# A gated mix of a state-space convolution and a GLU: the planner orders the queues with another timing model

## The chip, the cores and the metric

The kernel runs on one core of a Trainium2 chip. The metric is the device time of one execution in microseconds, from three runs of the kernel before: 757.71, 754.04 and 754.38, median 754.38. A core has five engines, each with a queue of its own that it works through in order: TensorE (PE in the profile; PEld is its loading of weights), VectorE (DVE), ScalarE (ACT), GpSimd (POOL) and SyncE (SP), which here issues every DMA transfer.

## The reference

The input `x` has 2048 positions (L) of 512 channels (D). Two branches are computed from it and mixed with a gate.

```
g = sigmoid((x * gate_w).sum(-1, keepdims=True))          # one number per position

# branch A: a convolution with a kernel built from a state space
dt = exp(log_dt)[:, None]                                 # 512 x 1
P  = exp((dt * (A_re + 1j*A_im))[:, :, None] * l)         # 512 x 128 x 2048, l = 0..2047
K  = einsum("dn,dnl,dn->dl", C_re + 1j*C_im, P, dt * (B_re + 1j*B_im)).real
y  = irfft(rfft(pad(x)) * rfft(pad(K)))[:2048] + x * Dskip   # per channel

# branch B: a GLU with 1792 hidden units
h  = sigmoid(x @ w_gate) * (x @ w_up)                     # 2048 x 1792
b  = h @ w_down                                           # 2048 x 512

out = g * y + (1 - g) * b
```

## The kernel before, in words

Branch A is done as matrix products in two stages, so that a transform of 4096 points becomes products with small constant matrices. Branch B is a plain chain of two matrix products whose operands are each split into a high and a low part (three products for one), for precision.

**kgen** (lines 191 to 241) builds the convolution kernel K in 16 rounds of 32 channels. A round takes the bases of the powers (`bases`, lines 147 to 178: products on VectorE, and Exp and Sin on ScalarE, lines 162 to 172), writes the first powers into the tile `T` (lines 200 to 204; `T` has one buffer, so a round can write it only when the `kps` products of the round before have read it), and then doubles the table of powers again and again (`double`, lines 180 to 189). A doubling is three operations on VectorE: two products (lines 187 and 188) and a sum (line 189), up to 128 x 2048 elements each. When the table is full, 128 small products on TensorE (line 220, tile `kps`) sum over the states, ScalarE copies the result (line 223, `kst`), VectorE adds Dskip (line 225), 32 products (line 232) make the first transform stage, and ScalarE copies these out (line 236). Every fourth round stores its result (line 239).

**rows** (lines 354 to 371) runs 16 times, once for each block of 128 positions. It loads the block, computes the gate (lines 360 to 362) and does the first transform stage of x on TensorE (line 367), which goes to a buffer in memory (line 371).

**glu** (lines 303 to 352) is a generator of the whole of branch B, so that the other parts can draw work from it in portions. It goes through two halves of the positions, four groups of hidden tiles (4, 4, 3 and 3 tiles of 128 units), two blocks of 512 positions. `load_x` (line 304) loads and splits x; `weights` (line 373) loads and splits one hidden tile's weights (casts on ScalarE, lines 381 and 382; low parts on VectorE, lines 384 and 385, stored for the second half in lines 386 and 387 and read back in lines 389 and 390); four weight tiles are held (`bufs=4`). `hidden` (line 393) makes one hidden tile for 512 positions: 24 products on TensorE (line 401) into two of three `gups` buffers, then a sigmoid on ScalarE (408), a product on VectorE (409), a cast on ScalarE (410) and the low part on VectorE (411). The second products (line 339) sum a group's hidden tiles into `dps`, and ScalarE or VectorE adds this to an accumulator (lines 343 and 345).

**finish** (lines 252 to 285) is the second transform stage in 16 passes: it loads four tiles (lines 255 to 261), makes products with the transformed x and with the transformed kernel (line 248), multiplies them (lines 268 and 269), combines and moves the parts (lines 274 to 278), makes the inverse products (line 281) and stores the result (line 284). **final** (lines 287 to 297) runs 16 times: it loads a block back, does the last stage (line 293), mixes it with branch B (line 296) and stores the output.

The program text (lines 426 to 457) interleaves these parts by hand-set step counts: `ROW` = 32 portions of `glu` for every four `rows`, `MID` = 50 for every half round of `kgen`, `END` and `LAST` for `finish` and `final`.

That text is not yet the order on the queues. The tile context collects all instructions and then plans them when its block closes: it plays the program through on a timing model, and at each moment gives an engine an instruction whose inputs are ready and whose buffers are free, and among those the one that stands first in the program text. Lines 214 to 240, from the `kps` products to the store, are raised above this with `tc.high_priority()`. The order in which the planner hands out the instructions is the order in which they stand on each engine's queue; on the chip each then waits for its own inputs. The timing model's times serve for this order alone.

## Time and profile before

| | |
|---|---|
| median of three runs | 754.38 us |
| the profiled execution | 753.36 us |
| its span, first to last instruction | 751.6 us |
| mean granted TensorE clock | 0.975 of full speed |
| instructions in the profile | 12658 |
| `kps` products, first and last start | 64.4 and 547.9 us |
| first products of `finish` (line 248) on the chain | 565.21 us |

The page gives busy times of each engine over the span. A fp32 matrix product appears as more than one record. The windows view gives, for stretches of the span, busy time and count of instructions of each engine, the granted TensorE clock, the share of DMA time and GB/s; asked for one source line it gives that line's instructions alone. The lines view groups instructions by source line and form: busy time and mean duration, then idle time of that engine just ahead of them, with what ended it. The chain that ended last gives in order of time the start, the length and the name of each piece that set the end. The waits view gives who waited for whom. A row named SPq is the DMA-issuing queue of SyncE.

### The profile page before, as it was taken

What the parts mean: (1) busy time and instruction counts of PE and PEld (TensorE: products, weight loads), DVE (VectorE), ACT (ScalarE), POOL (GpSimd) and SP (SyncE); (2) the same over time, 40 slices, a digit from 0 to 9 for tenths busy, and PEclk for the clock granted to TensorE, in tenths of its full rate; (3) what the DMA queues carried; (4) which work ended last, traced back from release to release, by engine and by line L of the source; (5) the groups of instructions that cost most, each with busy time, mean ns of one, the idle gap of its engine ahead of it and who ended that gap; (6) DMA issues with size and microseconds to landing.
All of it is one profiled execution on the core that took longest, in us unless ns stands there. A gap on an engine that the chain in (4) does not pass through costs nothing.

```text
span 751.6 us, 12658 instructions
## 1 busy us (share of the span) xinstructions
PE 706.8 (94%) x5024; PEld 475.2 (63%) x5024; DVE 604.9 (80%) x835; ACT 375.5 (50%) x611; POOL 3.7 (0%) x36
## 2 busy tenths in 40 slices
PE   4988889998999999999999999999999999999995
PEld 3445348877888778877787787887883323333651
DVE  5888989999999999899999898999944544454343
ACT  5364645763638274655565654546134555555200
POOL 0000000000000000000000000000000000000000
PEclk9789879999999999999999999999999999999999
DMA  6768662433025033565013350531158877774587
GB/s 221 213 204 229 170 178 97 156 104 148 32 88 183 22 115 130 194 237 175 26 57 126 100 189 8 168 115 56 57 187 284 258 241 243 225 223 147 174 285 254
DMA packets 61019, 118.64 MB, mean 158 GB/s; under 512 B 8224, under 2 KB 22944, under 8 KB 59936
## 3 DMA queue, kind: packets, MB, share of 16 engines
q1 hardware_dynamic: 60960, 117.84, 48.3%
q8 instruction: 39, 0.64, 0.3%
q14 instruction: 20, 0.16, 0.1%
HBM read 75.35 MB, written 42.47 MB: 157 GB/s over the span
## 4 chain that ended last, share of the span: by engine, by line
PE 53%; DVE 28%; ACT 8%; DMA 7%; issue 3%; SPq 0%; DVEq 0%; ACTq 0%
PE gups L401 19%; PE dps L339 12%; PE fps L248 9%; DVE T L189 6%; DVE T L188 6%; DVE tmp L187 6%; PE ips L281 4%; PE fps L367 3%; DVE h L409 2%; PE kps L220 2%; DVE hl L411 2%; DMA xs<-xt 2%; PE fps L232 2%; DMA wst<-wgu 1%; PE fps L293 1%
## 5 line engine op out<-in xcount | busy, mean ns | idle before, releaser
L401 PE MATMUL gups<-xh,gu 128*128 128x512 f32 x896 | 293.9, 402 | 15.2 <-ACT gu L381 12.5
L401 PEld LDWEIGHTS gups<-xh,gu 128*128 128x128 f32 x896 | 170.0, 191 | 71.4 <-issue 16.2
L401 PE MATMUL gups<-xl,gu 128*128 128x512 f32 x448 | 179.2, 400 | 0.0
L339 PE MATMUL dps<-dnw,hh 128*128 128x512 f32 x448 | 150.2, 402 | 3.6 <-ACT hh L410 3.0
L187 DVE TENSOR_TENSOR tmp<-T,bz 128x64 f32<-128x64 f32 (+2 forms) x96 | 114.8, 1195 | 2.3 <-issue 0.2
L189 DVE TENSOR_TENSOR T<-T,tmp 128x64 f32<-128x64 f32 (+2 forms) x96 | 114.6, 1194 | 0.7
L188 DVE TENSOR_TENSOR T<-T,bz 128x64 f32<-128x64 f32 (+2 forms) x96 | 114.6, 1193 | 0.0
L339 PEld LDWEIGHTS dps<-dnw,hh 128*128 128x128 f32 x448 | 83.5, 189 | 37.5 <-issue 11.6
L401 PEld LDWEIGHTS gups<-xl,gu 128*128 128x128 f32 x448 | 85.6, 191 | 27.4 <-issue 10.3
L339 PE MATMUL dps<-dnw,hl 128*128 128x512 f32 x224 | 89.6, 401 | 3.0 <-DVE hl L411 1.7
L408 ACT ACTIVATE sg<-gups 128x512 f32<-128x512 f32 x56 | 33.5, 598 | 70.3 <-PE gups L401 69.6
L268 DVE TENSOR_TENSOR t<-fps,uf 128x512 f32<-128x512 f32 x32 | 22.0, 688 | 57.6 <-PE fps L248 47.6
L410 ACT ACTIVATE hh<-h 128x512 fp32r<-128x512 f32 x56 | 35.1, 628 | 47.9 <-DVE h L409 47.9
L409 DVE TENSOR_TENSOR h<-gups,sg 128x512 f32<-128x512 f32 x56 | 38.1, 684 | 20.4 <-PE gups L401 20.1
L339 PEld LDWEIGHTS dps<-dnw,hl 128*128 128x128 f32 x224 | 42.3, 189 | 16.5 <-DVE hl L411 3.7
L411 DVE TENSOR_TENSOR hl<-h,hh 128x512 fp32r<-128x512 f32 x56 | 38.3, 686 | 8.9 <-ACT hh L410 8.4
L381 ACT ACTIVATE gu<-wst 128x1024 fp32r<-128x1024 f32 x28 | 29.6, 1057 | 29.4 <-PE gups L401 13.8
L345 DVE SCALAR_TENSOR_TENSOR acc<-dps,omg,acc 128x512 f32<-128x512 f32 x48 | 35.5, 746 | 10.3 <-PE dps L339 10.3
L248 PE MATMUL fps<-au,w_in 128*64 128x512 f32 x128 | 42.3, 611 | 0.3 <-DVE t L268 0.3
L236 ACT ACTIVATE kev<-fps 128x256 f32<-128x256 f32 x64 | 33.8, 678 | 16.3 <-PE fps L232 15.4
L248 PE MATMUL fps<-ak,w_in 128*64 128x512 f32 x128 | 41.2, 609 | 0.0
L367 PE MATMUL fps<-u,wu 64*128 64x512 f32 x64 | 32.4, 780 | 6.6 <-DMA u<-xp 2.9
(78 smaller groups left out, 664.5 us busy)
## 6 DMA issues: line engine op xcount, KB each, us to landing
wst<-wgu SPq DMA_DIRECT2D x28, 512.0 KB, 4.5
a_u<-evu SPq DMA_DIRECT2D x32, 256.0 KB, 3.3
a_k<-kev SPq DMA_DIRECT2D x8, 1024.0 KB, 6.0
au<-a_u SPq DMA_DIRECT2D x16, 512.0 KB, 4.8
ak<-a_k SPq DMA_DIRECT2D x16, 512.0 KB, 4.2
b_s<-evb SPq DMA_DIRECT2D x32, 256.0 KB, 2.5
b_in<-b_s SPq DMA_DIRECT2D x16, 512.0 KB, 4.6
wsd<-wdn SPq DMA_DIRECT2D x28, 256.0 KB, 3.5
```

The lines of the kernel that those rows point to most:

```text
L187: nc.vector.tensor_tensor(t2, src, sb, op=OP.mult)
L188: nc.vector.tensor_tensor(dst, src, br, op=OP.mult)
L189: nc.vector.tensor_tensor(dst, dst, t2[:, :, ::-1], op=OP.add)
L236: nc.scalar.activation(kv[i][:, s:s + 4], p4[:, :, :, 16 * i:16 * i + 16], AF.Copy)
L248: mm(p[64 * kb:64 * kb + 64], w[:, kb, 64 * c:64 * c + 64], a(kb), start=True, stop=True, tile_position=(0, 64 * kb), skip_group_check=True)
L339: mm(p, a[:, hs], dnw[:, b], start=(n == 0), stop=(n == last))
L345: nc.vector.scalar_tensor_tensor(accs[t], p, omg[:, t:t + 1], accs[t], op0=OP.mult, op1=OP.add)
L367: mm(ph[jp], wu[r, jp], u[r], start=True, stop=True, tile_position=(64 * jp, 0))
L401: mm(p, gu[:, a, k, dc], b[:, dc], start=(n == 0), stop=(n == 11))
L409: nc.vector.tensor_tensor(h, pp[1], sg, op=OP.mult)
L410: nc.scalar.activation(hh, h, AF.Copy)
L411: nc.vector.tensor_tensor(hl, h, hh.bitcast(F32), op=OP.subtract)
```

## The change

The tile context gets an argument that sets the timing model with which it plans. Without it, the planner uses a simple model with one cost for each instruction and transfer. With it, it uses a more detailed model, in which an instruction passes through its queue, its engine and the end of its writes one after another, and transfers through issue, start and data. Ranking, dependencies, buffers, the instructions themselves and what they compute stay as they are; the order on every queue, and with it the waits between them, can be another.

```
-    with tile.TileContext(nc) as tc, ExitStack() as ctx:
+    with tile.TileContext(nc, schedule_with_timeline_sim=True) as tc, ExitStack() as ctx:
         body(ctx, tc, *args)
```

## The prediction

> **What bounds the kernel now.** I read the page's totals first, then the busy times of three stages, then the chain that ended last for the pitch of each kind of product, then the waits.
>
> ```profile
> span 751.6 us, 12658 instructions
> PE 706.8 (94%) x5024; PEld 475.2 (63%) x5024; DVE 604.9 (80%) x835; ACT 375.5 (50%) x611; POOL 3.7 (0%) x36
> ```
>
> TensorE carries the span, but busy is not the same as working at full pitch. The stages come from the windows view (columns: stretch, its length, busy time of each engine with its instruction count, granted clock, DMA share): the head with the 16 `rows` steps, the middle with most of `kgen`, and the end with `finish` and `final`.
>
> ```profile
> 0.00:125.00 125.00, 100.40 (x587) 59.51 (x588) 105.93 (x183) 62.18 (x123) 0.84 (x10) 0.86 0.66 194
> 125.00:550.00 425.00, 414.30 (x3772) 335.75 (x3773) 408.86 (x515) 234.10 (x356) 2.82 (x26) 1.00 0.33 112
> 550.00:751.60 201.60, 192.06 (x672) 79.92 (x666) 90.07 (x138) 79.25 (x132) 0.00 (x0) 0.99 0.71 232
> ```
>
> The middle is a double bound: TensorE 414 and VectorE 409 of 425 us. In the end VectorE needs only 90 of 201.6 us. The same view for the GLU's products alone, line 401 first and line 339 second:
>
> ```profile
> 0.00:125.00 125.00, 46.28 (x155) 32.33 (x156) 0.86 0.66 194
> 125.00:550.00 425.00, 244.18 (x1032) 192.07 (x1031) 1.00 0.33 112
> 550.00:751.60 201.60, 45.42 (x158) 28.11 (x158) 0.99 0.71 232
> ...
> 0.00:125.00 125.00, 14.76 (x48) 9.31 (x48) 0.86 0.66 194
> 125.00:550.00 425.00, 128.27 (x516) 94.66 (x516) 1.00 0.33 112
> 550.00:751.60 201.60, 29.33 (x108) 19.42 (x108) 0.99 0.71 232
> ```
>
> The chain, in order of time (start, length, what), gives the pitch of undisturbed runs of products:
>
> ```profile
> 77.52 1.47 PE fps L367 x4
> 399.35 1.92 PE kps L220 x128
> 402.64 1.97 PE fps L232 x32
> 449.97 4.08 PE dps L339 x18
> 565.21 3.81 PE fps L248 x16
> 574.32 1.09 PE ips L281 x2
> 720.23 1.87 PE fps L293 x8
> ```
>
> So one GLU product takes 4.08/18 = 0.2267 us, and its 1344 + 672 = 2016 of them 457.0 us. The others: 16 rounds of `kps` at 1.92 (30.7) and of L232 at 1.97 (31.5), 64 of L367 at 0.3675 (23.5), 256 of L248 at 0.238 (61.0), 64 of L281 at 0.545 (34.9), 64 of L293 at 0.234 (15.0). Together 653.6 us, so 98 us of the span are lost by TensorE. By stage: the head has 203 GLU products (46.0), L367 (23.5) and two rounds of `kgen` (7.8), 77.3 of 125, and loses 47.7. The middle has 1548 (350.9) and 14 rounds (54.5), 405.4 of 425, and loses 19.6. The end has 266 (60.3) and 110.9 of `finish` and `final`, 171.2 of 201.6, and loses 30.4. A new order can win or lose only in these 98 us and in what it adds to them.
>
> **The change part by part.** It adds and removes no operation. The planner's timing model decides which ready instruction stands next on each queue, so all five queues can be written in another order; the queues then run in that order whatever the true times are. The trace of before shows no instruction of the new order, so each step below is a bound from the nearest rows.
>
> *Short jobs of `kgen` on TensorE.* Each of 16 rounds needs its `kps` products as soon as the last L189 ends, because the next round writes into the one buffer `T`. The timeline of one round:
>
> ```profile
> 198.69 2.28 DVE L189 TENSOR_TENSOR T<-T,tmp 128x2048 f32<-128x2048 f32 x1
> 201.51 1.99 PE L220 MATMUL kps<-T 128*32 128x64 f32 x128
> 204.16 0.21 DVE L200 TENSOR_TENSOR T<-w 128x32 f32<-128x32 f32 x1
> ```
>
> `kps` starts 0.54 us after L189 ends and the next round's L200 0.66 us after `kps`: today's order is nearly ideal here. The waits view (who waited for whom: us in total, times, longest) agrees; under it, the first and last start of the `kps` products:
>
> ```profile
> DVE T L200 <- PE kps L220: 7.1, 4, 1.9
> ...
> L220 PE MATMUL kps<-T x2048: 216/219/315, 64.4 to 547.9; 128*32 128x64 f32 x187
> ```
>
> A planner that commits TensorE's queue further ahead, or thinks the products sooner or later done than they are, puts `kps` behind GLU products that were ready first. Lower bound: nothing, or the gain of those 7.1 us. Upper bound: the rest of one hidden tile, 24 x 0.2267 = 5.4 us a round, 15 x 5.4 = 81 us. The cover, VectorE's GLU work, is no cover in the middle, since VectorE has 16 us free in 425. I take two thirds of the upper end, 3.6 us a round or 54 us, because the present order already sits at the lower end and has hardly anything left to win there.
>
> That stretch is not lost outright: TensorE fills it with GLU products taken from the end stage, whose 60.3 us shrink to 6.3. What the end then costs comes from its own two parts:
>
> ```profile
> 562.00:702.00 140.00, 139.43 (x448) 49.73 (x447) 67.62 (x107) 72.19 (x121) 0.00 (x0) 1.00 0.70 224
> 702.00:751.60 49.60, 40.63 (x159) 20.61 (x157) 18.82 (x26) 3.62 (x6) 0.00 (x0) 0.97 0.76 261
> ...
> 702.00:751.60 49.60, 14.48 (x59) 10.35 (x57) 0.97 0.76 261
> ...
> 702.00:751.60 49.60, 9.38 (x36) 6.45 (x36) 0.97 0.76 261
> ```
>
> Now 16 passes of `finish` take 140 us, 8.75 each. Without GLU between them a pass needs 6.0 us of TensorE ((61.0 + 34.9)/16) and 6.1 of DMA (0.70 x 8.75), and its steps wait for one another; I take 7.5, midway, 120 us. After 702, 95 GLU products (21.5) drop out and leave 28.1. With the 12 us from 550 to 562 the end is 160.1 instead of 201.6, 41.5 less. Sum: +54.0 - 41.5 = +12.5 us.
>
> *The GLU's elementwise steps on VectorE.* L409 and L411 are ranked against the long doublings of `kgen`, and ScalarE's L408 and L410 stand between them:
>
> ```profile
> L187 DVE TENSOR_TENSOR tmp<-T,bz 128x2048 f32<-128x2048 f32 x32 | 73.1, 2285 | 0.2
> ACT sg L408 <- PE gups L401: 69.6, 25, 12.4
> ```
>
> Here ScalarE mostly waits for TensorE (69.6 us), not the reverse, so results are taken off in time. One spare of three `gups` buffers is 12 products, 2.7 us. Bounds: no loss; or, if both VectorE steps stand behind one more 2.2 us doubling, 4.4 - 2.7 = 1.7 us for each of the middle's 43 hidden tiles (1032/24), 73 us. I take nothing, near the present row; the upper end is a rival.
>
> *ScalarE's table loads.* Their number depends on how Exp, Sin and Sigmoid interleave.
>
> ```profile
> L408 ACT ACT_TABLE_LOAD x22 | 28.2, 1283 | 0.7 <-PE gups L401 0.4
> L167 ACT ACT_TABLE_LOAD x16 | 20.5, 1283 | 0.3
> L165 ACT ACT_TABLE_LOAD x15 | 19.2, 1283 | 0.2
> ```
>
> A round needs Exp, Sin and back, so 16 rounds need about the 53 shown. Ten fewer to thirty more are -13 to +38 us of ScalarE, which has 191 us free in the middle: nothing on the path. Where that cover fails, one load costs 1.28 us ahead of one sigmoid.
>
> *The DMA queue.* All transfers stand on SP's one queue; a store that waits holds the loads behind it.
>
> ```profile
> SPq L386 <- DVE gu L384: 77.5, 10, 26.2
> ACT gu L381 <- DMA wst<-wgu: 13.5, 10, 3.1
> ```
>
> The store of line 386 holds that queue up to 26.2 us, yet the weight cast waited only 13.5 us for loads in all, since four weight tiles are held. Bounds: a gain of 13.5; or a loss of as much again if loads slip behind another store. I take zero. POOL has two memsets a round and `T`'s release sets them: they go with the first step.
>
> *The head.* The order of `rows`, `load_x` and the first GLU tiles is open to gain, which is a rival.
>
> Sum: 751.6 + 12.5 = 764.1 us of span. The profiled execution took 753.36 us, 1.8 more than its span, and the median of the runs, 754.38, is 1.0 above it: 764.1 + 1.8 + 1.0 = 767.
>
> **The rivals.** *The head gets better (faster).* The head loses 47.7 us: TensorE idles 24.6 and the clock of 0.86 costs 0.14 x 125 = 17. Truer transfer times in the planner could place `rows` and loads better. But the doublings must follow, and VectorE is idle only 19 us of the head, so that is the most the middle can move up. With three quarters of it, 14 us, and no `kps` delay: 754 - 14 = 740 (735 to 750; with the middle's idle time also halved, 8 us, 728). For it: the head is the one place with slack. Against it: no wait there is longer than a few us, and the order's step counts (`ROW`, `MID`) were not re-cut for a new order.
>
> *The GLU starves (much slower).* One mechanism: L409 and L411 behind another doubling each. It decides once that delay passes the 2.7 us spare. Half the price above, 36 us, gives 790; the whole 827. Against it: today's 69.6 us of ScalarE waiting for TensorE must first be used up.
>
> *The end runs cold.* If the end loses its GLU filling and TensorE's clock falls to the head's 0.86, its 110.9 us cost 110.9/0.86 - 110.9 = 18 more: 785. For it: the head, with waits between its matmuls, shows 0.86 where the middle shows 1.00. Against it: 6.0 us of work in a pass of 7.5 leaves gaps of at most 1.5. [...] No row of before shows the end without its GLU filling, so the small chance stays.
>
> *The order hardly changes what matters.* Both models may give the same broad order, `kps` first and GLU between: 751 to 758.
>
> **How the numbers follow.** The late `kps` 0.38, the cold end 0.05, starving 0.11, the better head 0.34, no change 0.12. About 0.5% is what a measurement of this kernel tells from no change, so under 750.6 is faster and over 758.2 slower: faster 0.34, same 0.12, slower 0.54. The likeliest case gives 767; its own range is 754 (delay zero) to 794 (81 - 41.5 = 39.5). Cases of both signs count, so the range goes from the better head with a better middle, 728, to most of the starving case, 818; about 0.06 lies beyond each end.
>
> **What would show it.** Late `kps`: VectorE's wait of L200 for `kps` grows from 7.1 to some 50 us, the last `kps` moves from 547.9 to about 600, fewer than 266 GLU products remain after it, and passes of `finish` come faster than 8.75 us. Wrong, if that wait stays under 15 us. Better head: the windows row of the first 125 us shows more than 203 GLU products and a clock above 0.86. Starving: TensorE waits for L408 or L411 for tens of us. Cold end: a clock below 0.95 after the last `kps`. The table loads are right if between 45 and 90 and ScalarE stays under 450 us. The forecast fails altogether if the new order changes the number of switches between the kinds of products, which costs TensorE time within its busy share and which I priced at nothing.

## The result and the profile after

The changed kernel takes 819.93 us (median of four runs, 819.33 to 824.03) against 756.05 us of the kernel before on the same chip: 1.085 times as long, with an interval of 1.078 to 1.091. The prediction had 767 us, 1.7% above the 754.38 from which it started. The sign was right; the loss is 64 us and not 12.5, and the time lies just above the range's upper end of 818.

The page's totals of the changed kernel, then the windows view cut where the last `kps` products start, whole first, then for lines 401 and 339 alone:

```profile
span 822.1 us, 12692 instructions
PE 713.1 (87%) x5024; PEld 486.4 (59%) x5024; DVE 605.5 (74%) x835; ACT 382.4 (47%) x617; POOL 3.7 (0%) x36
...
0.00:125.00 125.00, 84.39 (x484) 48.13 (x485) 95.63 (x173) 58.51 (x111) 0.83 (x10) 0.78 0.58 177
125.00:638.00 513.00, 494.66 (x4099) 403.35 (x4101) 437.55 (x549) 253.31 (x389) 2.84 (x26) 0.98 0.30 99
638.00:822.10 184.10, 134.04 (x454) 34.95 (x444) 72.28 (x113) 70.61 (x117) 0.00 (x0) 0.80 0.76 250
...
0.00:125.00 125.00, 29.05 (x100) 20.89 (x101) 0.78 0.58 177
125.00:638.00 513.00, 298.44 (x1246) 234.53 (x1244) 0.98 0.30 99
638.00:822.10 184.10, 0.00 (x0) 0.00 (x0) 0.80 0.76 250
...
0.00:125.00 125.00, 14.88 (x48) 9.89 (x48) 0.78 0.58 177
125.00:638.00 513.00, 159.29 (x624) 117.30 (x624) 0.98 0.30 99
638.00:822.10 184.10, 0.00 (x0) 0.00 (x0) 0.80 0.76 250
```

The busy times of the engines moved by 2.4% at most, but all three stages look different. The head holds 148 GLU products instead of 203, at a clock of 0.78 instead of 0.86. VectorE, which was busy for 409 of 425 us in the middle, is now busy for 438 of 513. The end has no GLU product left and a clock of 0.80.

The first and last start of the `kps` products, and the waits that grew:

```profile
L220 PE MATMUL kps<-T x2048: 219/219/314, 71.2 to 638.7; 128*32 128x64 f32 x187
...
PEld fps L367 <- ACT evu L368: 30.8, 7, 7.0
DVE T L200 <- PE kps L220: 29.5, 10, 4.7
DVE o L296 <- DMA out<-o: 27.5, 13, 2.5
PE fps L367 <- ACT evu L368: 23.0, 7, 5.4
ACT evu L368 <- DMA a_u<-evu: 14.5, 5, 6.2
...
PE gups L401 <- ACT sg L408: 9.4, 4, 3.7
```

The last `kps` moved from 547.9 to 638.7. In the kernel before, L367 waited 2.5 us in all for L368 on TensorE, and L368 only 0.6 us for the stores of `evu`:

```profile
PE fps L367 <- ACT evu L368: 2.5, 2, 1.8
...
ACT evu L368 <- DMA a_u<-evu: 0.6, 2, 0.3
```

One round of the changed kernel in the timeline:

```profile
451.26 2.28 DVE L189 TENSOR_TENSOR T<-T,tmp 128x2048 f32<-128x2048 f32 x1
...
455.49 0.69 DVE L411 TENSOR_TENSOR hl<-h,hh 128x512 fp32r<-128x512 f32 x1 [1.95 <-ACT hh L410]
458.37 0.69 DVE L411 TENSOR_TENSOR hl<-h,hh 128x512 fp32r<-128x512 f32 x1 [1.59 <-ACT hh L410]
459.11 1.83 PEld L220 LDWEIGHTS kps<-T 128*32 128x32 f32 x128 [0.35 <-issue]
459.11 1.99 PE L220 MATMUL kps<-T 128*32 128x64 f32 x128
461.17 0.22 DVE L200 TENSOR_TENSOR T<-w 128x32 f32<-128x32 f32 x1 [2.11 <-PE kps L220]
```

The table is full at 453.54, and `kps` starts at 459.11, 5.57 us late; behind L189 VectorE has three short GLU steps to do (the third, L409, stands between the two shown) and idles 5.65 us (1.95, 1.59 and 2.11) until L200. In the round of the kernel before that the prediction shows, the same gap was 0.54 us. Over 16 rounds this lateness (end of the last L189 to the start of `kps`) adds up to 72.0 us, where it was 7.1.

The span splits like this (the head's share is the price that two runs below give it):

| | predicted | measured |
|---|---|---|
| head | 0 | +22 |
| middle, to the last `kps` | +54.0 | +68.8 (638.7 - 547.9 = 90.8, less the head's 22) |
| from the last `kps` to the end | -41.5 | -20.3 (203.7 to 183.4) |
| sum | +12.5 | +70.5 (822.1 - 751.6) |

The spans shown differ by 70.5 us, the medians by 63.9.

### The profile page after: what moved, and what is told of

Same layout as the page of the kernel before. It is cut to its first block, busy times and chain, and to the rows that moved or that the text cites. A ratio compares the mean times of both kernels' runs of the same rounds, so it can differ in the third digit from the quotient of the medians.

```text
span 822.1 us, 12692 instructions
## 1 busy us (share of the span) xinstructions
PE 713.1 (87%) x5024; PEld 486.4 (59%) x5024; DVE 605.5 (74%) x835; ACT 382.4 (47%) x617; POOL 3.7 (0%) x36
## 4 chain that ended last, share of the span: by engine, by line
PE 46%; DVE 22%; DMA 16%; ACT 11%; issue 4%; SPq 1%; DVEq 0%; ACTq 0%
PE gups L401 21%; PE dps L339 9%; PE fps L248 5%; DVE tmp L187 5%; DVE T L188 5%; DVE T L189 4%; DMA wst<-wgu 4%; DMA wsd<-wdn 4%; PE ips L281 3%; DMA out<-o 3%; PE kps L220 3%; PE fps L232 2%; DVE acc L345 2%; PE fps L367 2%; DMA a_u<-evu 1%
## 5 line engine op out<-in xcount | busy, mean ns | idle before, releaser
L401 PE MATMUL gups<-xl,gu 128*128 128x512 f32 x448 | 177.1, 395 | 0.0
L339 PE MATMUL dps<-dnw,hh 128*128 128x512 f32 x448 | 152.5, 404 | 6.0 <-DVE acc L345 5.8
L189 DVE TENSOR_TENSOR T<-T,tmp 128x64 f32<-128x64 f32 (+2 forms) x96 | 114.8, 1195 | 0.8
L339 PEld LDWEIGHTS dps<-dnw,hh 128*128 128x128 f32 x448 | 86.1, 193 | 29.9 <-DVE acc L345 6.9
L367 PE MATMUL fps<-u,wu 64*128 64x512 f32 x64 | 33.4, 807 | 27.4 <-ACT evu L368 23.0
L408 ACT ACTIVATE sg<-gups 128x512 f32<-128x512 f32 x56 | 33.5, 597 | 44.7 <-PE gups L401 44.5
L411 DVE TENSOR_TENSOR hl<-h,hh 128x512 fp32r<-128x512 f32 x56 | 38.2, 684 | 16.2 <-ACT hh L410 16.1
L381 ACT ACTIVATE gu<-wst 128x1024 fp32r<-128x1024 f32 x28 | 29.6, 1057 | 37.7 <-PE gups L401 19.8
L248 PE MATMUL fps<-au,w_in 128*64 128x512 f32 x128 | 34.5, 637 | 14.0 <-issue 13.2
L293 PE MATMUL fps<-b_in,wf 128*64 128x512 f32 x64 | 27.8, 975 | 20.7 <-DMA b_in<-b_s 11.1
L281 PE MATMUL ips<-y,wv 128*128 128x512 f32 x64 | 38.2, 680 | 6.8 <-ACT y L278 4.8
L409 DVE TENSOR_TENSOR h<-gups,sg 128x512 f32<-128x512 f32 x56 | 38.3, 684 | 6.8 <-PE gups L401 4.6
```

The lines of the kernel that those rows point to most:

```text
L189: nc.vector.tensor_tensor(dst, dst, t2[:, :, ::-1], op=OP.add)
L248: mm(p[64 * kb:64 * kb + 64], w[:, kb, 64 * c:64 * c + 64], a(kb), start=True, stop=True, tile_position=(0, 64 * kb), skip_group_check=True)
L281: mm(p, wv[:, kb], y[:, kb], start=True, stop=True)
L339: mm(p, a[:, hs], dnw[:, b], start=(n == 0), stop=(n == last))
L367: mm(ph[jp], wu[r, jp], u[r], start=True, stop=True, tile_position=(64 * jp, 0))
L401: mm(p, gu[:, a, k, dc], b[:, dc], start=(n == 0), stop=(n == 11))
```

## The experiments

For each kernel I work out what TensorE loses in three stretches: the length of a stretch less the products counted in it, each by the pitch of the prediction. The losses are those of the one execution that was profiled, which can lie up to 6 us from the median in the second column. The runs are explained below; the table is for looking back.

| kernel | time, us | ratio | lost in first 150 us | from 150 to last `kps` | after last `kps` | late `kps`, sum | GLU products left |
|---|---|---|---|---|---|---|---|
| before | 756 | 1 | 48 | 20 | 30 | 7 | 270 |
| changed | 820 | 1.085 | 71 | 27 | 71 | 72 | 0 |
| n_hold | 821 | 1.087 | 71 | 45 | 49 | 42 | 270 |
| b_late | 830 | 1.099 | 46 | 50 | 78 | 127 | 0 |
| n_nohp | 824 | 1.090 | 61 | 45 | 64 | 67 | 0 |
| n_pinPE | 836 | 1.105 | 75 | 64 | 40 | 59 | 270 |
| n_pinSP | 830 | 1.099 | 71 | 27 | 82 | 74 | 62 |
| n_pinVA | 839 | 1.111 | 56 | 88 | 38 | 61 | 264 |
| b_pinPE | 869 | 1.149 | 72 | 74 | 68 | 181 | 0 |
| n_freePE | 847 | 1.122 | 58 | 89 | 45 | 62 | 264 |
| n_freeDVE | 824 | 1.089 | 73 | 65 | 31 | 92 | 270 |
| n_pre150 | 798 | 1.056 | 54 | 22 | 68 | 53 | 0 |
| b_pre150 | 777 | 1.029 | 66 | 23 | 30 | 13 | 270 |
| n_pre550 | 773 | 1.024 | 54 | 20 | 48 | 7 | 270 |
| n_evupair | 804 | 1.063 | 59 | 24 | 65 | 63 | 0 |
| n_oneload | 802 | 1.060 | 70 | 26 | 53 | 72 | 0 |

### Is it the place of `kps` on TensorE's queue?

My theory was the prediction's: GLU products stand ahead of `kps`. The first run lets the new planner order everything, but a GLU product that stood behind a round's `kps` in the kernel before may not be handed out ahead of it. In the trace this takes hold from the seventh round on, where about as many GLU products stand ahead of `kps` as before; the first six rounds keep the places of the changed kernel. The edge carries no semaphore; it only binds the order.

```
+PLACE = [107, 144, 258, 375, 489, 620, 746, 879, 1004, 1120, 1209, 1311, 1425, 1536, 1644, 1746]
...
+    def prod(*a, **k):
+        x = mm(*a, **k)
+        PROD.append(x)
+        r = [q for q, n in zip(KPS, PLACE) if n < len(PROD)]
+        if r:
+            after(x, r[-1])
+        return x
```

> The new timing model, but the kps products of each round get back, by added order edges on TensorE, nearly the place among the GLU products that they had before (at most 114 GLU products a round instead of 144 from round 6 on); everything else stays as the new model plans it. Late-kps theory: kps follows T within 1 us from about round 6 on, the last kps ends near 575 instead of 639, some 270 GLU products are left for the end stage, and the time falls to 770 (760 to 785); the rest above 756 is the head, which is not touched. Rival (the new order costs through its other parts: VectorE, ScalarE, the DMA queue, the end): the time stays above 805.

Measured: 821.23 us, 1.087 [1.079, 1.094]: a miss. The lateness fell from 72 to 42 us, the last `kps` ends at 595 instead of 639, 270 GLU products stay for the end, and not one microsecond is gained. What was won ahead of the last `kps` was paid behind it. With their old places back, single rounds still come 4 to 5 us late, so this run gives back the place of `kps` and only a part of its time.

The reverse, under the old planner: `kps` is tied behind as many GLU products as stand ahead of it in the changed kernel (116, 144, 229, 366, ... 2016).

```
+    for r, n in enumerate(PLACE):
+        after(KPS1[r], PROD[n - 1])
```

> The old timing model, with one added order edge a round: kps may not stand ahead of the GLU product that it follows in the new order (144 a round). Nothing else is forced. Late-kps theory: the middle stretches by some 60 to 70 us, GLU runs out at its end, the time is 805 (795 to 820). Rival (other parts of the new order cost the time): below 775.

Measured: 830.08 us, 1.099 [1.089, 1.109], with a good head, but above the expected 795 to 820: `kps` is late by 127 us in sum here and not by 72. So a late `kps` is enough to cost as much as the change, at more lateness than the change has, and yet taking its place back does not give that back. The third run takes away the raised rank of lines 214 to 240:

```
-            hp = tc.high_priority(); hp.__enter__()
...
-            hp.__exit__(None, None, None)
```

> The new timing model without the raised rank of the block from kps to the store. If kps is late because TensorE's queue is filled about 20 products ahead of time, rank does not matter much once the round runs: kps still follows T by some 5 us, the middle's rounds stay near 37 us and the time is within 2% of 820. Rival (kps is late because it is outranked): its lateness grows to 10 us or more a round and the time to 860 or more.

Measured: 823.76 us, 1.090 [1.079, 1.102] from two runs. `kps` starts late by 67 us in sum; in the first two rounds its products now stand scattered among others. The rank is not what decides.

### Is it one queue?

The next runs hold whole queues in the order that they have in the other kernel. `ORDER` lists the instructions of a queue as they stand there:

```
+    here = {i.name: i for i in nc.cur_bb.bb.instructions}
+    info = mybir.DependencyInfo(mybir.DependencyClass.NoSync, mybir.DependencyReason.DATA)
+    for queue in ORDER.values():
+        for a, b in zip(queue, queue[1:]):
+            tc.add_manual_dep(here[f"I-{b}"], f"I-{a}", info, reason="order")
```

TensorE's queue as before, the rest by the new planner:

> The new planner, with TensorE's queue held in the order of the kernel before (each matrix product is tied to stand behind the one that stood ahead of it there); the other queues are left to the new planner. Theory A, TensorE's order is the cause: the time returns to 756 to 770, the sum of late kps to under 20 us, the last kps to about 550, the first 150 us to some 49 us of loss. Rival B, the order of the DMA queue and of VectorE and ScalarE is the cause: the time stays above 800.

Measured: 835.78 us, 1.105 [1.100, 1.111]. The DMA queue as before:

> The new planner, with SyncE's DMA queue alone held in the order of the kernel before. Theory A (TensorE's order): 805 to 825, kps late by some 70 us in sum as in the changed kernel, last kps past 620. Rival B (the DMA queue is the cause, above all in the head): under 790, and the first 150 us hold more GLU products than the changed kernel's 211.

Measured: 829.88 us, 1.099 [1.093, 1.106]. VectorE's and ScalarE's queues as before:

> The new planner, with the queues of VectorE and ScalarE held in the order of the kernel before; TensorE's and the DMA queue's are left to the planner, whose TensorE order moves with them, about half way back. Theory A (TensorE's order): 770 to 800, and the time follows how far kps stands back at its place. Rival B' (the order on VectorE and ScalarE is the cause): 752 to 762. Rival B'' (neither matters): 815 to 825.

Measured: 839.46 us, 1.111 [1.105, 1.118]. The old planner with TensorE's queue as in the changed kernel:

> The old planner, with TensorE's queue held in the order of the changed kernel; the other queues are left to the old planner. Theory A (TensorE's order): 812 to 825, the changed kernel's whole loss, with kps late by 60 to 80 us in sum and the 16 final steps behind all of finish. Rival B: under 790.

Measured: 869.28 us, 1.149 [1.143, 1.155]. The last three times lie outside every range put down for them. Theory A falls, and with it every theory that blames one queue: with the old order put back on one queue, or on two, the kernel is slower than with the new order on all queues. In `n_pinPE` not one GLU product more stands ahead of `kps` than before, and still `kps` is 59 us late in sum.

So I formed theory C: an order is good or bad for all queues together, and a queue that is out of step with the others costs as much as a whole new order. Two runs test it by letting a single queue go. TensorE's alone (in the trace a product stands some 30 places from its old one on average):

> The new planner, with the queues of VectorE, ScalarE and the DMAs held in the order of the kernel before; TensorE's queue alone is ordered by the new planner (each product stands 26 places from its old one on average). Theory C, any one queue out of step with the others costs as much as all: 825 to 845, as with the DMA queue free too (839). Rival F, the DMA queue's order had a part in that: under 800.

Measured: 847.35 us, 1.122 [1.116, 1.128], 2 us above the range of theory C. VectorE's alone:

> The new planner, with the queues of TensorE, ScalarE and the DMAs held in the order of the kernel before; VectorE's queue alone is ordered by the new planner (1.5 places from its old one on average, 20 at most). If the time hangs on the places themselves, so small a shift costs little: 754 to 775. Theory C, a queue out of step with the others costs as much as all of them moved, however small the shift: over 800.

Measured: 824.05 us, 1.089 [1.083, 1.095], where VectorE's instructions are shifted by 1.6 places on average in the trace, and TensorE's and ScalarE's stand where they stood. Its waits (line 533 is line 339 of the kernel before, 394 is 200, 554 is 360, 602 is 408):

```profile
ACT sg L602 <- PE gups L595: 88.0, 27, 17.4
...
DVE T L394 <- PE kps L414: 19.0, 10, 3.8
...
DVE ju L554 <- DMA u<-xp: 15.7, 6, 7.8
...
PE dps L533 <- ACT hh L604: 12.6, 5, 5.5
...
PE dps L533 <- DVE hl L605: 11.7, 8, 2.9
```

In the kernel before the last three read:

```profile
PE dps L339 <- ACT hh L410: 3.0, 3, 1.8
DVE ju L360 <- DMA u<-xp: 2.1, 2, 1.4
PE dps L339 <- DVE hl L411: 1.7, 2, 1.4
```

None of these waits of TensorE and VectorE grew by more than 14 us. I read them as a ring: VectorE stands for a block of x that has not landed, TensorE then for a `hl` that is behind on VectorE, VectorE for `kps` behind TensorE's backlog. The sums fit this, but no run shows that one wait brings on the next. TensorE loses 25 us more than before in the first 150 us and 45 more in the middle; there TensorE was busy 97% of the time and VectorE 96% in the kernel before, so little is left to catch up with.

### What each stage costs

If the order counts as a whole, it can still be cut in time. Here all four queues are held in the order of the kernel before for what had started there by 150 us, and everything else is tied behind that:

```
+    for engine, queue in ORDER.items():
+        for a, b in zip(queue, queue[1:]):
+            tc.add_manual_dep(here[f"I-{b}"], f"I-{a}", info, reason="order")
+        for n in REST[engine]:
+            tc.add_manual_dep(here[f"I-{n}"], f"I-{queue[-1]}", info, reason="order")
```

> The new planner, but every queue (TensorE, VectorE, ScalarE, DMA) is held in the order of the kernel before for what had started there by 150 us; only behind that the new planner orders freely. The changed kernel loses 21.7 us more of TensorE in its first 150 us. Theory D, the stages add up (each stage's loss is its own): 798 (790 to 806), with the head's row as before and the later rounds as in the changed kernel. Rival E, a good head only lets the later rounds run into the same limit: over 812.

Measured: 797.83 us, 1.056 [1.050, 1.062]. The reverse, the old planner behind the changed kernel's head:

> The reverse of the first: the old planner, with all four queues held in the order of the changed kernel for what had started there by 150 us; behind that the old planner orders freely. Theory D: 756 + 22 = 778 (770 to 786). Rival E: the old order behind it makes the head good again by filling the end less: under 765; or a bad head puts TensorE behind VectorE for good and kps comes late in the later rounds too: over 790.

Measured: 776.84 us, 1.029 [1.024, 1.035]. And the old order up to 550 us:

> The new planner, with all four queues held in the order of the kernel before for what had started there by 550 us; the new planner orders only the end (finish, final and the last 270 GLU products). Theory D: the last kps at 548 and a total of 770 to 780, because the end ordered by the new planner took 222 us instead of 203 where it had as many GLU products left (the run that held the GLU back). If the end is as good as before: 752 to 760. If the end is the main cause: over 790.

Measured: 772.63 us, 1.024 [1.018, 1.030]. All three times fell where theory D put them (the last `kps` of `n_pre550` ended at 554, not 548). The head is worth 22 us both ways (1.085 - 1.056 and 1.029 - 1); the end, alone, 18 (0.024 x 755); the middle what lies between `n_pre150` and `n_pre550`, 1.056 - 1.024 = 0.032, or 24 us. That the three make up the whole loss of 64 is no test, since each is a difference along one line from the changed kernel to the kernel before. The test is that the head has the same price in both directions. Nor is it the added order edges that cost: `n_pre550` holds all four queues by them for 550 us and loses 54 and 20 us in its first two stretches, where the kernel before loses 48 and 20.

`n_hold` agrees from another side: against the kernel before TensorE loses 22, 24 and 19 us more in its three stretches. In the changed kernel itself the middle shows only 7 us more and the stretch behind it 41. I read this so: where `kps` comes late, the GLU's products fill the middle, TensorE's loss moves from there to an end without filling, and the sum stays.

### The head

The wait that grew most there is TensorE's for L368, and behind it ScalarE's for the stores of `evu` (two buffers). One buffer now takes two blocks, so that four blocks can wait for their store in the same space:

```
-        ev = pp.tile([P, 2, D], F32, tag="kev", bufs=2, name="evu")
+        if t % 2 == 0:
+            W["ev"] = pp.tile([P, 2, 2, D], F32, tag="kev", bufs=2, name="evu")
+        ev = W["ev"][:, t % 2]
```

> The changed kernel, with each buffer of the row results (evu) taking two blocks, so that four of them can wait for their store instead of two. Theory I, the head's extra 21.7 us come from ScalarE standing still for these stores (14.5 us) and TensorE behind it: the wait of L368 for the store under 4 us, TensorE's loss in the first 150 us from 69 to 50 to 55, the total 798 to 806. Rival J, the head's loss is spread over the whole order and not in this one wait: over 812.

Measured: 803.89 us, 1.063 [1.059, 1.066], 16 us less than the changed kernel. L368 no longer waits for these stores; of TensorE's 23 us more in the head 12 are gone (71 to 59, where 50 to 55 were expected). The edit also moves the order on the queues, so that the 16 us need not be the wait's alone. The first 125 us of this run:

```profile
0.00:125.00 125.00, 90.33 (x527) 50.54 (x527) 96.59 (x176) 63.57 (x119) 0.83 (x10) 0.84 0.61 189
```

The same edit in the kernel before, where ScalarE waits 0.6 us in all for the stores:

> The kernel before, its planner unchanged, with each buffer of the row results (evu) taking two blocks, as in the run of the changed kernel that gained 16 us by it. In the kernel before ScalarE does not wait for these stores, so there is little to take away: 750 to 757. A gain of the size seen in the changed kernel (740) would mean that the stores held the head there too; above 760, that a shift of the order costs here as it does with the new planner.

Measured: 766.36 us, 1.012 [1.007, 1.017]: a miss on the bad side. A wait that was hardly there could not be taken away, but the edit changed the order, and the head's first 125 us fell to a clock of 0.78 (TensorE's loss in the first 150 us from 48 to 61):

```profile
0.00:125.00 125.00, 96.30 (x542) 54.71 (x543) 100.61 (x177) 61.53 (x119) 0.84 (x10) 0.78 0.62 182
```

### The end

After the last pass of `finish` come 16 bare `final` steps. In windows, the two parts of the changed kernel's end, and two finals on VectorE:

```profile
656.00:770.00 114.00, 101.59 (x320) 26.04 (x320) 60.20 (x96) 67.49 (x112) 0.00 (x0) 0.93 0.82 264
770.00:822.10 52.10, 27.80 (x64) 4.91 (x64) 11.91 (x16) 0.42 (x1) 0.00 (x0) 0.60 0.74 247
...
800.97 0.75 DVE L296 SCALAR_TENSOR_TENSOR o<-fps,g,acc 128x512 f32<-128x512 f32 x1 [1.79 <-DMA out<-o]
803.92 0.75 DVE L296 SCALAR_TENSOR_TENSOR o<-fps,g,acc 128x512 f32<-128x512 f32 x1 [2.21 <-DMA out<-o]
```

Most finals wait for a store (27.5 us in 13 waits). First the output buffers:

```
-        o = pp.tile([P, D], F32, tag="o", bufs=2, name="o")
+        o = pp.tile([P, D], F32, tag="o", bufs=4, name="o")
```

> The new timing model with four instead of two buffers for the output tile o of final. If the pace of the last 16 steps (2.7 us each after 776 us) is set by o waiting for its store (27.5 us of waits), they take about 2.0 each and the time falls by 8 to 14 us, to 808. Rival (the pace is set by the loads b_in on the one DMA queue): within 3 us of 820.

Measured: 816.71 us, 1.080 [1.072, 1.087]: a miss, with 3 us that the intervals do not even separate from nothing. The waits for stores are gone, but VectorE now waits for L293 instead (37.6 us for 17.0); from the last product of `finish` to the end it is 47.0 us for 52.3. Then the transfers: one load of 512 KB serves all 16 finals. The run leaves out the other 15 loads and what they bring, so it tells what the time hangs on and is no kernel to use.

```
-        b = pp.tile([P, 2, D], F32, tag="big", bufs=3, name="b_in")
-        nc.sync.dma_start(b, b_s[8 * m:8 * m + 8].rearrange("(j r) k d -> (r k) j d", j=2))
+        if m == 0:
+            W["b"] = pp.tile([P, 2, D], F32, tag="big", bufs=3, name="b_in")
+            nc.sync.dma_start(W["b"], b_s[8 * m:8 * m + 8].rearrange("(j r) k d -> (r k) j d", j=2))
+        b = W["b"]
```

> The changed kernel, but the 16 final steps load their 512 KB input once, for the first of them, and all use it (15 loads and what they bring are left out; the order of the products is the same). Theory G, the bare finals are paced by their transfers (768 KB each at some 280 GB/s are 2.7 us): they come 1.0 to 1.6 us apart, the tail is 18 to 26 us shorter, the total 794 to 804. Rival H, TensorE at its lower clock or the two output buffers set the pace: over 812.

Measured: 802.3 us, 1.060 [1.056, 1.064], 18 us less than the changed kernel. Its tail, and two of its finals, 1.5 us apart:

```profile
770.00:802.00 32.00, 18.96 (x64) 4.02 (x64) 12.02 (x16) 0.00 (x0) 0.00 (x0) 0.82 0.40 147
...
782.20 0.75 DVE L298 SCALAR_TENSOR_TENSOR o<-fps,g,rst 128x512 f32<-128x512 f32 x1 [0.75 <-DMA out<-o]
783.68 0.75 DVE L298 SCALAR_TENSOR_TENSOR o<-fps,g,rst 128x512 f32<-128x512 f32 x1 [0.73 <-DMA out<-o]
```

The bare finals are paced by their transfers: 52.1 us at 247 GB/s are 12.9 MB, and 16 loads of 512 KB and 16 stores of 256 KB are 12.6. The kernel before needs the same transfers, and its finals took 49.7 us with 95 GLU products among them. So the 18 us of `n_oneload` show what bounds the finals; they are not what the change cost there.

The 18 us that the new order of the end costs alone lie elsewhere. These are the 16 passes of `finish` and then the finals, in the kernel before and in `n_pre550`:

```profile
565.20:701.90 136.70, 136.13 (x433) 47.32 (x433) 66.87 (x106) 71.87 (x119) 0.00 (x0) 1.00 0.69 221
701.90:751.60 49.70, 40.73 (x159) 20.66 (x158) 18.82 (x26) 3.69 (x6) 0.00 (x0) 0.97 0.76 262
...
573.20:723.60 150.40, 144.10 (x515) 59.71 (x514) 75.21 (x118) 74.53 (x123) 0.00 (x0) 0.99 0.62 200
723.60:775.00 51.40, 28.80 (x64) 4.99 (x64) 12.02 (x16) 0.60 (x1) 0.00 (x0) 0.57 0.74 250
```

Less the 320 records of the passes and the 64 of the finals, these rows count GLU products: the new planner takes all 95 out of the finals and has 195 among the passes, where there were 113. The finals get no shorter by it, since their transfers stay, and the passes, in which TensorE was busy all the time already, get 14 us longer.

The output buffers in the kernel before:

> The kernel before with four output buffers in place of two (its planner unchanged). Its final steps wait 5.1 us for their stores in sum: 748 to 755 if that wait sets the end, no change if the transfers do. Theory G: no change that can be measured (752 to 757).

Measured: 756.13 us, 1.003 [0.999, 1.006], no change that can be measured. No run beats the kernel before.

## Why the prediction was right or wrong

**Late `kps`: the mechanism was seen, the size was a little low, and it is not the lever.** I put it at 3.6 us a round, 54 in sum. With the head taken out (`n_pre150`) the lateness sums to 53 us, in the changed kernel to 72. VectorE's wait for it (29.5 us) is under the "some 50" named and above the 15 that would have refuted it, because GLU steps stand between, and part of VectorE's idling is put down to ScalarE ahead of these. "The last `kps` at about 600" was 638.7, 22 of that from the head; "fewer than 266 products behind it" was none. But the middle became 69 us longer, not 54, and `n_hold` shows that putting `kps` back at its old place from the seventh round on returns nothing. I took one queue's place as the cause from which the rest follows; the runs show that in this kernel the queues only work as one order.

**The end: the step that failed most clearly.** "After 702, 95 GLU products drop out and leave 28.1" took TensorE as the limit of the finals. They took 52 us. The row that I had quoted said so: 49.6 us at 261 GB/s are 12.9 MB, the finals' own transfers, with the GLU hidden beneath them. Taking a hidden load away shortened nothing. My sum also had no place for the 6.3 us of GLU products that it left for the end; none were left. Of the rest, 120 us for the 16 passes were 113 (656.8 to 770), better than thought, and the 12 us ahead of them were 18, with the load of `a_k` waiting for its last store. In sum -20 instead of -41.5.

**The head: taken at nothing, with a gain as its rival, and it lost 22.** I had argued that no wait there is longer than a few us and saw only what could be won. Two waits were longer: TensorE's of 9.8 us for L381 and ScalarE's of 10.3 us for L367. And short waits bear the opposite reading too: a stretch that is held together by them can be made worse by a new order. The two row buffers were one such place (23.0 us of TensorE's waits for L368 where there were 2.5); about half of TensorE's loss there came back with them, and what the rest hangs on stays open. I gave the head no bound on the losing side.

**Starving GLU.** Its sign, TensorE waiting for L408 or L411 for tens of us, did not come in the changed kernel (9.4 us for L408); in `n_freeDVE`, with the old TensorE order, TensorE's waits for `hh` and `hl` rose from 4.7 to 24.3 us in sum. As a rival for the change it was wrong.

**The cold end** was half right: the clock after the last `kps` is 0.80, below the 0.95 named. The passes of `finish` held 0.93, with pauses of under 0.9 us but for two of 2.0. The finals ran at 0.60, and with 15 loads gone (`n_oneload`) at 0.82. Whether the low clock has a price of its own is not settled: `b_late`, whose end has no GLU products either, took 46.5 us from the last product of `finish` at a clock of 0.72, against 52.3 in the changed kernel, so that up to 6 us may be the clock's. That gaps of at most 1.5 us speak against a low clock was my estimate, and the runs do not settle it: the finals from 788 to 808 us had pauses of 0.57 to 1.10 us at a clock of 0.50.

**ScalarE's tables** came out as put: 65 loads for 59, ScalarE at 382 us. The switches between GLU products and all others on TensorE's queue, a number that I had said would unmake the forecast if it changed, fell from 169 to 83. Behind `kps` in the kernel before, the first GLU product starts 0.34 us ahead of the next (203.43 and 203.77), where the pitch is 0.2267. If the fewer switches saved anything, it does not show, as TensorE's busy time rose from 706.8 to 713.1.

**The chances.** "Slower" had 0.54 and came. The range went to most of the starving case, and that it came within 2 us of the measured time is luck: late `kps` with a lost head and a tail set by transfers was no case of mine.

What stays open: which feature of the more detailed model makes its order worse. The runs tell what the order costs and where, not why the model prefers it; the middle's 24 us in particular are only a difference between two runs. That a planned order without the two row buffers' wait and with the old end would beat the kernel before was not shown either.

## What to carry to other kernels

In a kernel whose two main engines are 96 to 97% busy, treat the queues as one order: here, holding or moving one of them cost as much as a new order of all (ratios of 1.089 to 1.149 against 1.085), so test an order whole, or cut it in time, not by engine. Before a stage is shortened by the work that leaves it, multiply its GB/s by its length: if that is what its own transfers need, the work is probably hidden, and its leaving gains nothing, as here (12.9 MB moved, 12.6 of them the finals' own, and the finals took 52.1 us after 49.7). A stretch with only short waits is a risk as much as a reserve: the head lost 22 us.

## What the runs showed of the hardware

The finals of the changed kernel had a granted clock of 0.60 over their 52.1 us, and of 0.50 from 788 to 808 us, where the pauses between their products were 0.57 to 1.10 us. TensorE's timeline, and the windows rows of the same stretch, of 8 us and of 1 us:

```profile
776.87 4.88 PE L293 MATMUL fps<-b_in,wf 128*64 128x512 f32 x12 [7.09 <-DMA b_in<-b_s]
782.85 1.08 PE L293 MATMUL fps<-b_in,wf 128*64 128x512 f32 x4 [1.09 <-DMA b_in<-b_s]
786.00 1.08 PE L293 MATMUL fps<-b_in,wf 128*64 128x512 f32 x4 [2.07 <-DMA b_in<-b_s]
787.95 1.98 PE L293 MATMUL fps<-b_in,wf 128*64 128x512 f32 x4 [0.87 <-DMA b_in<-b_s]
...
801.77 1.98 PE L293 MATMUL fps<-b_in,wf 128*64 128x512 f32 x4 [0.57 <-DVE o L296]
...
776.00:784.00 8.00, 5.96 (x16) 1.50 (x16) 1.99 (x3) 0.00 (x0) 0.00 (x0) 0.68 0.80 247
784.00:792.00 8.00, 4.34 (x12) 0.85 (x12) 1.76 (x3) 0.00 (x0) 0.00 (x0) 0.75 0.95 342
800.00:808.00 8.00, 5.45 (x14) 0.89 (x12) 2.25 (x3) 0.00 (x0) 0.00 (x0) 0.50 0.88 295
...
780.00:781.00 1.00, 1.00 (x4) 0.27 (x2) 0.41 (x1) 0.00 (x0) 0.00 (x0) 0.50 0.84 209
781.00:782.00 1.00, 0.75 (x4) 0.00 (x0) 0.34 (x1) 0.00 (x0) 0.00 (x0) 0.95 1.01 301
...
787.00:788.00 1.00, 0.13 (x4) 0.09 (x3) 0.38 (x1) 0.00 (x0) 0.00 (x0) 0.97 1.04 401
788.00:789.00 1.00, 1.00 (x4) 0.24 (x4) 0.00 (x0) 0.00 (x0) 0.00 (x0) 0.50 1.02 373
```

Four of these records took 1.08 us where the clock was 1.00 (782.85 and 786.00) and 1.98 us where it was 0.50 (787.95 and 801.77). The first twelve ran 4.88 us without a pause; the clock was 0.50 from 777 to 781 us and 0.95 in the row from 781 to 782. It was 1.00 from 782 to 787 and 0.97 from 787 to 788, and from 788 to 808 it was 0.50; the pauses up to there were 1.09, 2.07 and 0.87 us. In `n_oneload` 20 records ran 7.09 us without a pause, and the groups of four behind them took 1.08 us each, with pauses of 0.33 to 0.43 us; the row from 775 to 800 us has a clock of 0.91:

```profile
773.99 7.09 PE L295 MATMUL fps<-b_in,wf 128*64 128x512 f32 x20 [6.59 <-DMA b_in<-b_s]
786.00 1.08 PE L295 MATMUL fps<-b_in,wf 128*64 128x512 f32 x4 [0.43 <-DVE o L298]
```

What sets the clock was not shown: between these stretches the pauses, the bursts and the transfers all differ.
